# Moving the key sums, the PE transposes and the last batch's transposes of an attention + gated convolution kernel

## The chip, the cores and the metric

One core of a Trainium2 chip runs the whole program. The metric is device time in microseconds (us) for one execution, lower is better. The engines are TensorE (PE, with its weight loads shown apart as PEld), VectorE (DVE), ScalarE (ACT), GpSimd (POOL) and SyncE (SP, which here issues every DMA). Each engine works through its own queue in order.

## The reference

Attention of 12288 queries on 768 pooled keys per batch (4 batches, 128 channels), and behind it a causal 5-tap convolution that gates a projection.

```
kv_flat = mean of kv over 4 x 4 blocks, @ w_sr      # (B, 768, 128); k = v = kv_flat
s = (q @ k^T) / sqrt(128);  a = softmax(s);  x = a @ v            # (B, 12288, 128)
gate = sigmoid(sum_k conv_w[k] * x shifted by 4 - k rows)
out = (gate * (x @ w_val)) @ w_out
```

The inputs are float32 except the last weights, which can come as float64 and are then converted on DVE in 14 short steps.

## The kernel before, in words

The queries are cut into 96 groups of 512 (24 per batch), each group into four tiles j = 0 to 3 of 128 queries. The main loop runs over t = 4 * group + j and writes every engine's instructions out in that order (the order is by hand; nothing is rescheduled). At step t the current group `cur` has its softmax, while earlier groups are further on: `last` (one back) gets its normalisation row, `avg` (two back) is multiplied with the values, `xg` (three back) is convolved, `mg` (four back) is gated and projected, `og` (five back) is stored.

Per group, with the short names that the prediction uses:

- S, `score`: six matmuls that make the scores of the next tile in PSUM (three buffers, tile `s`). q and the keys are split in two parts (qh, ql and kh, kl), hence three products on two halves.
- nm, `row_max` (DVE): the negated maximum of a tile. Then `expo` (ACT), the exponential, with the row sums in z.
- `p_hi` (ACT) and `p_lo` (DVE): the exponentials as two float16 parts. For tiles 0 to 2 they go to `hl`, and DMA transposes turn them into `pt` (tiles 0 and 1 together, tile 2 alone). Tile 3 goes another way: `expo` writes it to `pf`, six PE transposes ("turns", T; T1 is the first) put it back in PSUM turned round, and `p_hi`, `p_lo` write `pt` directly.
- AV, `av_part`: 18 matmuls of `pt` with the values into one PSUM bank `av`, cut over the four steps by AV_CUTS. Then `g_x` (DVE) makes x from it, with the row `rb` of reciprocals that went by way of DRAM (`norm_turn` on PE into the bank `m`, `norm_store` copies it to r and stores rd, `norm_rows` loads rb). POOL copies the four halo columns of x first, behind `g_ql`.
- `g_qh` (ACT) and `g_ql` (POOL), at j = 2: the two parts of q for the group after the next.
- V, `g_val`: x times w_val, at j = 1, into the same single bank `m` that r was read from. h, `g_h` (DVE): (tanh + 1) times V. O, `g_out`: h times w_out, at j = 2. The convolution, `g_conv`, is on POOL but for one tap on ACT; `g_evac` on ACT writes the output tile.

The keys of the next batch are made beside the groups of the current one by `setup_steps`: one step a group, at j = 3. A step is a function that may return two more, `high` and `low`, which the loop calls at j = 0 of the next group. For 16 groups a step loads a piece of kv (the first step loads three) and its `low` is `pool_kv`, a DVE sum over the 16 pixels of a block; then come two steps of `project` (with the copies kh and vt as `high`, kl as `low`), and five of `value_steps` (the column scale, dripped over several steps by `trickle`, and the values vh and vl).

Behind the loop the last five groups n5 to n1 are finished in an order of their own, the last two with the convolution on DVE (`conv_dve`), the very last in two halves.

Of the kernel before, what the change touches and what calls it, by code (L numbers as in the profile page):

```python
# [6 lines left out]
F32 = mybir.dt.float32  # L7
# [20 lines left out]
def attn_moe_kernel(ctx, tc, qT, kvT, w_sr, w_moe, outT):  # L28
# [10 lines left out]
    TAPS = NW - 2 * C  # L39
    HALO = TAPS - 1  # L40
    PIECES = 16
    AV_CUTS = (0, 7, 9, 12, 18)
    assert 3 * NCH == AV_CUTS[-1]
    PC = NK // PIECES
    AHEAD = 5
# [17 lines left out]
    def misc():  # L63
        return ps_m.tile([P, GQ], F32, name="m")
# [55 lines left out]
    def pool_kv(st, i):  # L120
        nc.vector.tensor_reduce(out=st["pool"][:, i * PC:(i + 1) * PC],  # L121
                                in_=st.pop(("kv", i)).rearrange("c (k s) -> c k s", s=RR),
                                axis=AX.X, op=ALU.add)
# [77 lines left out]
    def setup_steps(b, st):  # L201
        def piece(i):
            if i == 0:
                key_tiles(st)
            for k in range(3) if i == 0 else (i + 2,):
                if k < PIECES:
                    load_kv(b, st, k)
            return None, lambda: pool_kv(st, i)

        steps = [lambda i=i: piece(i) for i in range(PIECES)]  # L210
        steps += [lambda h=h: project(st, h, misc()) or split_keys(st, h) for h in range(2)]
        return steps + value_steps(st)

# [27 lines left out]
    def halves(a):  # L241
        return a.rearrange("p (h k) -> p h k", h=2)
# [13 lines left out]
        nc.vector.tensor_reduce(out=nm, in_=g.s[j], axis=AX.XY, op=ALU.max, negate=True)  # L256
        g.nm[j] = nm

    def on_pe(j):

        return j >= NX

    def expo(g, j):
        if j == 0:
            g.z = zs[g.i % len(zs)]
        if on_pe(j):
            g.pf[j] = pfp.tile([P, NK], F32, name="pf")
        nc.scalar.activation(out=halves(g.pf[j]) if on_pe(j) else g.s[j], in_=g.s[j],  # L268
                             func=AF.Exp, bias=g.nm.pop(j), accum_out=g.z[:, j:j + 1])

    def norm_eps(g):
# [21 lines left out]
    def turn(g, j):  # L293

        pf = g.pf.pop(j)
        for k in range(NCH):
            c = k % (NCH // 2) * P
            nc.tensor.transpose(g.s[j][:, k // (NCH // 2), c:c + P], pf[:, k * P:(k + 1) * P],  # L298
                                ident)
# [5 lines left out]

    def part(g, j, a):

        if on_pe(j):
            return pt_tile(g)[:, j, a * NCH:(a + 1) * NCH].rearrange("p (h k) q -> p h (k q)", h=2)
        if g.hl is None:  # L310
            g.hl = hlp.tile([P, NX, 2, NK], F16, name="hl")
        return halves(g.hl[:, j, a])

    def p_hi(g, j):
# [2 lines left out]
    def p_lo(g, j):  # L317

        nc.vector.scalar_tensor_tensor(out=part(g, j, 1), in0=g.s.pop(j), scalar=2.0 ** 15,  # L319
                                       in1=part(g, j, 0), op0=ALU.mult, op1=ALU.subtract)  # L320
        if j in (1, 2):
            j0 = 0 if j == 1 else j
            nc.sync.dma_start_transpose(
                out=pt_tile(g)[:, j0:j + 1].rearrange("p j k q -> p (j k) q"),
                in_=g.hl[:, j0:j + 1].rearrange("p j a k -> p (j a k)"))
# [6 lines left out]
            nc.tensor.matmul(out, g.st[v][:, k * P:(k + 1) * P], g.pt[:, j0:j1, a * NCH + k],  # L332
                             start=(i == 0), stop=(i == len(AV_ORDER) - 1))

    def av_part(g, part):
        if part == 0:
            g.av = ps_av.tile([C, GQ], F32, name="av")
        av_range(g, g.av, AV_CUTS[part], AV_CUTS[part + 1])

    def new_x(g, prev, copy):  # L340
        g.x = xp.tile([C, HALO + GQ], F32, name="x")
# [99 lines left out]
    for i in range(PIECES):  # L441
        if i + AHEAD < PIECES:
            load_kv(0, st, i + AHEAD)
        if i == 3:
            convert = load_moe()
        pool_kv(st, i)
        if i >= 8 and convert:
            convert.pop(0)()
        if i == 3 * PIECES // 4:
            low()  # L450
        if i % (PIECES // 2) == PIECES // 2 - 1:
            h = 2 * i // PIECES
# [17 lines left out]
    for t in range(NT * G):  # L470
        gi, j = divmod(t, NT)
        cur, prev, nxt = (at(u // NT) for u in (t, t - 1, t + 1))
        last, avg, xg, mg, og = (at(gi - d) for d in (1, 2, 3, 4, 5))
        if j == 2 and gi % 2 == 0 and at(gi + 4):
            load_pair(at(gi + 4), at(gi + 5))
        if gi % NG == 1 and j == 0 and at(gi + NG - 1):
            steps += setup_steps(cur.b + 1, states[cur.b + 1])
        if t == NT + 2:
            trickle += convert

        if nxt:
            score(nxt, (j + 1) % NT)
        if mg and j == 1:
            mg.m = g_val(mg, misc())
        if mg and j == 2:
            mg.m = g_out(mg.h, misc())
        if avg:
            av_part(avg, j)

        if high and (j == 0 or t < NT):  # L490
            high()
            high = None
        row_max(cur, j)
# [24 lines left out]
        drip()
        if mg and j == 1:
# [45 lines left out]
    new_x(n1, n2, nc.scalar.copy)
    avs = [bank()[:, :half] for _ in cuts]
# [5 lines left out]
    ths = []  # L572
    n1.th = work.tile([C, GQ], F32, name="th")
    for av, c in zip(avs, cuts):
        g_x(n1, av, *c)
        ths.append(g_tanh(conv_dve(n1, *c), n1.th[:, c[0]:c[1]]))
# [3 lines left out]
    n3.th = g_tanh(n3.gate)  # L580
    h = g_h(n3.th, n3.m)
    ms = [g_val(n1, bank()[:, :half], *c) for c in cuts]
    hs = [g_h(th, m) for th, m in zip(ths, ms)]
    n3.m = g_out(h, misc())
# [33 lines left out]
```

## Time and profile before

| | us |
|---|---|
| median of 3 runs | 1132.18 (1131.02 to 1132.25) |
| the profiled execution | 1133.22, its span 1131.4 |
| busy: PE, DVE, ACT, POOL | 1063.6, 919.0, 910.4, 864.4 |
| granted PE clock, mean | 0.983 |
| bytes moved by DMA | 215.53 MB, queue share 85.4% of 16 engines |

The span runs from the first instruction to the last; the profiled execution's time is 1.8 us longer than it. In rows of the timeline the columns are the start, the length, the engine, the line, the operation, output and input, the shape, and in brackets the idle time of the engine before it and what ended that idle time. In rows of the waits: who waited for whom, the total, the number of times and the longest. In rows of the chain of waits: start, length, engine, what is written, the line and the number of instructions. Matmuls are pipelined, so the lengths in the timeline overlap; the distance between starts is what PE spends.

### The profile page before, as it was taken

The numbers are of one execution on the slowest core, as the hardware profiler recorded it, in microseconds if no ns is written. First come the engines' busy times: TensorE is split into PE (matmuls) and PEld (weight loads), VectorE is DVE, ScalarE is ACT, GpSimd is POOL, SyncE is SP. The second block draws the span as 40 slices with busy tenths as digits, with TensorE's granted clock in tenths as the row PEclk, the third lists the DMA queues.
The fourth block names the chain that finished last, engine by engine and source line by source line (L and its number), as shares of the span: only waits on it lengthen the run. The fifth ranks groups of instructions, "written<-read, shape, count | busy, mean of one in ns | idle before, by whom it ended". The sixth has DMA issues, their size and how long they took to land.

```text
span 1131.4 us, 16595 instructions
## 1 busy us (share of the span) xinstructions
PE 1063.6 (94%) x5174; PEld 715.6 (63%) x5174; DVE 919.0 (81%) x1290; ACT 910.4 (80%) x1659; POOL 864.4 (76%) x948
## 2 busy tenths in 40 slices
PE   2879999999979999999997999999999999999996
PEld 1656666666756666666764666666666666666663
DVE  6868888888858888888885888888888888888884
ACT  1868888888858888888885888888888888888881
POOL 1168788878858888888885888887888888888872
PEclk9989999999989999999998999999999999999998
DMA  7779999887879999888876999898788888888872
GB/s 271 145 178 200 211 210 232 192 178 191 187 169 198 202 224 214 206 177 191 187 165 170 209 217 226 200 221 183 171 171 197 187 170 202 186 170 199 175 148 93
DMA packets 487095, 215.53 MB, mean 190 GB/s; under 512 B 453088, under 2 KB 453856, under 8 KB 487008
## 3 DMA queue, kind: packets, MB, share of 16 engines
q1 hardware_dynamic: 487008, 214.48, 85.4%
q8 instruction: 41, 0.67, 0.2%
q14 instruction: 46, 0.38, 0.1%
HBM read 75.83 MB, written 25.36 MB: 89 GB/s over the span
## 4 chain that ended last, share of the span: by engine, by line
PE 49%; DVE 25%; ACT 11%; issue 6%; POOL 5%; DMA 3%; SPq 1%; DVEq 0%; ACTq 0%
PE s L250 17%; PE av L332 16%; PE m L388 8%; DVE nm L256 8%; POOL ql L236 5%; ACT s L268 5%; DVE pool L121 4%; DVE pt L319 4%; ACT hl L315 4%; DVE x L349 4%; PE m L398 3%; PE s L298 3%; DMA kvt<-in_kv 3%; ACT qh L232 2%; DVE h L393 2%
## 5 line engine op out<-in xcount | busy, mean ns | idle before, releaser
L368 POOL TENSOR_TENSOR sum<-sum,tap 128x512 f32<-128x512 f32 x282 | 359.6, 1275 | 39.7 <-ACT tap L357 17.8
L332 PE MATMUL av<-pt,vh 128*128 128x512 f16 x1140 | 389.1, 383 | 0.0
L256 DVE TENSOR_REDUCE nm<-s 128x1 f32<-128x768 f32 x384 | 364.4, 949 | 3.7 <-PE s L250 3.7
L268 ACT ACTIVATE s<-s,nm 128x768 f32<-128x768 f32 x288 | 251.9, 875 | 125.5 <-DVE nm L256 124.3
L359 POOL TENSOR_SCALAR tap<-x,wm 128x512 f32<-128x512 f32 x376 | 253.4, 693 | 82.4 <-DVE x L349 80.9
L319 DVE SCALAR_TENSOR_TENSOR hl<-s,hl 128x768 f16<-128x768 f32 x288 | 273.1, 948 | 21.0 <-ACT hl L315 20.3
L250 PE MATMUL s<-kh,qh 128*128 128x384 f32 x768 | 253.3, 411 | 10.8 <-DVE hl L319 8.1
L315 ACT ACTIVATE hl<-s 128x768 f16<-128x768 f32 x288 | 233.3, 810 | 9.1
L332 PEld LDWEIGHTS <-vh 128*128 128x128 f16 x1164 | 114.0, 98 | 175.5 <-issue 85.8
L332 PE MATMUL av<-pt,vl 128*128 128x512 f16 x570 | 217.5, 382 | 0.0
L236 POOL TENSOR_TENSOR ql<-q,qh 128x512 fp32r<-128x512 f32 x96 | 121.8, 1269 | 122.6 <-ACT qh L232 122.6
L250 PE MATMUL s<-kh,ql 128*128 128x384 f32 x768 | 199.1, 341 | 0.0
L250 PE MATMUL s<-kl,qh 128*128 128x384 f32 x768 | 198.9, 340 | 0.0
L250 PEld LDWEIGHTS s<-kh,qh 128*128 128x128 f32 x768 | 132.4, 193 | 51.8 <-DVE hl L319 8.4
L349 DVE SCALAR_TENSOR_TENSOR x<-av,down,rb 128x512 f32<-128x512 f32 x95 | 71.4, 751 | 89.6 <-POOL ql L236 71.5
L250 PEld LDWEIGHTS s<-kl,qh 128*128 128x128 f32 x768 | 141.3, 190 | 0.5 <-DVE kl L147 0.5
L250 PEld LDWEIGHTS s<-kh,ql 128*128 128x128 f32 x768 | 140.9, 190 | 0.0
L388 PE MATMUL m<-x,wm 128*128 128x512 f32 x188 | 103.0, 630 | 25.0 <-DVE r L285 24.9
L368 POOL TENSOR_TENSOR sum<-tap,tap 128x512 f32<-128x512 f32 x94 | 120.4, 1281 | 0.0
L393 DVE SCALAR_TENSOR_TENSOR h<-th,m 128x512 f32<-128x512 f32 x94 | 64.7, 689 | 59.2 <-PE m L388 57.7
L315 ACT ACTIVATE pt<-s 128x768 f16<-128x768 f32 x96 | 77.8, 810 | 37.8 <-PE s L298 37.8
L332 PEld LDWEIGHTS <-vl 128*128 128x128 f16 x582 | 57.6, 99 | 77.9 <-issue 55.2
(68 smaller groups left out, 1068.9 us busy)
## 6 DMA issues: line engine op xcount, KB each, us to landing
kvt<-in_kv SPq DMA_DIRECT2D x64, 384.0 KB
rb<-rd SPq DMA_DIRECT2D x96, 256.0 KB
q<-in_q SPq DMA_DIRECT2D x47, 512.0 KB
out<-o SPq DMA_DIRECT2D x46, 512.0 KB
pt<-hl SPq DMA_TRANSPOSE x192
rd<-r SPq DMA_DIRECT2D x96, 2.0 KB
out<-o SPq DMA_DIRECT2D x3, 256.0 KB
q<-in_q SPq DMA_DIRECT2D x2, 256.0 KB
```

The lines of the kernel that those rows point to most:

```text
L236: nc.gpsimd.tensor_tensor(out=g.ql, in0=g.q, in1=g.qh.bitcast(F32), op=ALU.subtract)
L250: nc.tensor.matmul(s[:, h, :HALF], a[:, sl], k[:, h * HALF:(h + 1) * HALF], start=(i == 0), stop=(i == 2))
L256: nc.vector.tensor_reduce(out=nm, in_=g.s[j], axis=AX.XY, op=ALU.max, negate=True)
L268: nc.scalar.activation(out=halves(g.pf[j]) if on_pe(j) else g.s[j], in_=g.s[j], func=AF.Exp, bias=g.nm.pop(j), accum_out=g.z[:, j:j + 1])
L315: nc.scalar.activation(out=part(g, j, 0), in_=g.s[j], func=AF.Copy, scale=2.0 ** 15)
L319: nc.vector.scalar_tensor_tensor(out=part(g, j, 1), in0=g.s.pop(j), scalar=2.0 ** 15, in1=part(g, j, 0), op0=ALU.mult, op1=ALU.subtract)
L332: nc.tensor.matmul(out, g.st[v][:, k * P:(k + 1) * P], g.pt[:, j0:j1, a * NCH + k], start=(i == 0), stop=(i == len(AV_ORDER) - 1))
L349: nc.vector.scalar_tensor_tensor(out=g.x[:, HALO + c0:HALO + c1], in0=av, scalar=g.st["down"], in1=g.rb[:, c0:c1], op0=ALU.mult, op1=ALU.mult)
L359: eng.tensor_scalar(out=g.tap[k], in0=src, scalar1=w, scalar2=1.0, op0=ALU.mult, op1=ALU.mult)
L368: nc.gpsimd.tensor_tensor(out=s, in0=acc, in1=g.tap[k], op=ALU.add)
L388: nc.tensor.matmul(m, wval, g.x[:, HALO + c0:HALO + c1], start=True, stop=True)
L393: nc.vector.scalar_tensor_tensor(out=h, in0=th, scalar=1.0, in1=m, op0=ALU.add, op1=ALU.mult)
```

## The change

Six things are done at once.

1. `pool_kv` is no longer the `low` of its step. The next step puts it on a list, and the loop takes one from the list at j = 2, behind `p_lo`. There is one step more in a setup, 24 instead of 23.
2. `row_max` and `expo` are written ahead of AV, and the six turns of tile 3 are no longer issued in one run behind AV: `av_part` puts one behind each of its last six matmuls. AV_CUTS become (0, 6, 8, 10, 18): six, two, two and eight matmuls at j = 0 to 3 instead of seven, two, three and six.
3. As a consequence `high` (kh and vt, or vh) stands behind the exponential of tile 0 on ACT, not ahead of it.
4. In the last batch, groups with an even number have all four tiles turned by DMA, 0 with 1 and 2 with 3. They have no turns on PE; tile 3's `p_hi` and `p_lo` write to `hl`.
5. The 14 steps of the weight conversion all drip from step t = 3 on; before, eight stood between the key sums of the startup and six from t = 6 on.
6. Behind the loop, AV of the last but one group comes first, and tanh, h and output of the third last group stand between the two halves of the last one.

```
-    AV_CUTS = (0, 7, 9, 12, 18)
+    AV_CUTS = (0, 6, 8, 10, 18)
...
             if i == 0:
                 key_tiles(st)
+            else:
+                pooling.append(lambda: pool_kv(st, i - 1))
             for k in range(3) if i == 0 else (i + 2,):
                 if k < PIECES:
                     load_kv(b, st, k)
-            return None, lambda: pool_kv(st, i)
-        steps = [lambda i=i: piece(i) for i in range(PIECES)]
+        steps = [lambda i=i: piece(i) for i in range(PIECES + 1)]
...
-        if j in (1, 2):
-            j0 = 0 if j == 1 else j
+        if (j % 2 or j == g.by_dma - 1) and not on_pe(g, j):
+            j0 = j // 2 * 2
             nc.sync.dma_start_transpose(
...
-    def av_part(g, part):
+    def av_part(g, part, between=()):
         if part == 0:
             g.av = ps_av.tile([C, GQ], F32, name="av")
-        av_range(g, g.av, AV_CUTS[part], AV_CUTS[part + 1])
+        lo, hi = AV_CUTS[part], AV_CUTS[part + 1]
+        for i in range(lo, hi):
+            av_range(g, g.av, i, i + 1)
+            if hi - i <= len(between):
+                between.pop(0)()
+        for matmul in between:
+            matmul()
...
+            g.by_dma = 4 if b == B - 1 and i % 2 == 0 else 3
...
-        if i >= 8 and convert:
-            convert.pop(0)()
...
-        if t == NT + 2:
+        if t == 3:
             trickle += convert
...
+        row_max(cur, j)
+        expo(cur, j)
+        turns = turn_steps(cur, j) if on_pe(cur, j) else []
         if avg:
-            av_part(avg, j)
+            av_part(avg, j, turns)
+        else:
+            for matmul in turns:
+                matmul()
         if high and (j == 0 or t < NT):
             high()
             high = None
-        row_max(cur, j)
-        expo(cur, j)
-        if on_pe(j):
-            turn(cur, j)
+        if j == NT - 1:
             norm_eps(cur)
...
+        if pooling and j == 2:
+            pooling.pop(0)()
...
     norm_reciprocal(n1)
-    p_lo(n1, NT - 1)
-    store_pair(n5)
+    av_part(n2, 0)
     norm_turn(n1, misc())
     n4.th = g_tanh(n4.gate)
-    norm_store(n1)
-    n4.m = g_val(n4, misc())
-    av_part(n2, 0)
-    norm_rows(n1)
     tap(n3, TAPS - 1, nc.scalar)
     g_conv(n3)
-    h = g_h(n4.th, n4.m)
+    p_lo(n1, NT - 1)
+    norm_store(n1)
+    store_pair(n5)
     for i in (1, 2, 3):
         av_part(n2, i)
+    norm_rows(n1)
+    n4.m = g_val(n4, misc())
...
-    av_range(n1, avs[0], 0, len(AV_ORDER), 0, NT // 2)
-    h = g_h(n2.th, n2.m)
-    av_range(n1, avs[1], 0, len(AV_ORDER), NT // 2, NT)
-    n3.m = g_val(n3, misc())
-    n2.m = g_out(h, bank())
...
+    g_x(n1, avs[0], *cuts[0])
+    h2 = g_h(n2.th, n2.m)
+    n2.m = g_out(h2, bank())
+    ths = [g_tanh(conv_dve(n1, *cuts[0]), n1.th[:, :half])]
+    n3.m = g_val(n3, misc())
+    n3.th = g_tanh(n3.gate)
...
+    g_x(n1, avs[1], *cuts[1])
+    h3 = g_h(n3.th, n3.m)
...
+    ths.append(g_tanh(conv_dve(n1, *cuts[1]), n1.th[:, half:]))
```

On PE, at j = 3 of a group in the middle, before: the end of the last three of the six AV matmuls, the turns in one run, and the score of tile 1 of the next group (LDWEIGHTS loads the weights of the row behind it).

```order
L332 LDWEIGHTS vl
L332 MATMUL av<-pt,vl 128x512
L332 LDWEIGHTS vh
L332 MATMUL av<-pt,vh 128x512
L298 MATMUL s<-ident,pf 128x128 x6
L250 MATMUL s<-kh,qh 128x384 x2
L250 MATMUL s<-kl,qh 128x384 x2
L250 MATMUL s<-kh,ql 128x384 x2
```

And in the change, from the score of tile 0 on:

```order
L251 MATMUL s<-kh,ql 128x384 x2
L336 LDWEIGHTS vl
L336 MATMUL av<-pt,vl 128x512
L336 LDWEIGHTS vh
L336 MATMUL av<-pt,vh 128x512
L336 LDWEIGHTS vh
L336 MATMUL av<-pt,vh 128x512
L300 MATMUL s<-ident,pf 128x128
L336 LDWEIGHTS vl
L336 MATMUL av<-pt,vl 128x512
L300 MATMUL s<-ident,pf 128x128
```

The first turn stands behind three AV matmuls instead of six, and the last behind the last AV, with five AVs between first and last.

On DVE, one group of a batch in which the next batch's keys are summed, before: from the reciprocal at j = 0 to x at j = 3.

```order
L275 RECIPROCAL z_103<-z_103 128x4
L319 SCALAR_TENSOR_TENSOR pt<-s,pt 128x768
L121 TENSOR_REDUCE pool<-kvt 128x48
L256 TENSOR_REDUCE nm<-s 128x1
L285 COPY r<-m 4x128
L319 SCALAR_TENSOR_TENSOR hl<-s,hl 128x768
L393 SCALAR_TENSOR_TENSOR h<-th,m 128x512
L256 TENSOR_REDUCE nm<-s 128x1
L319 SCALAR_TENSOR_TENSOR hl<-s,hl 128x768
L256 TENSOR_REDUCE nm<-s 128x1
L319 SCALAR_TENSOR_TENSOR hl<-s,hl 128x768
L349 SCALAR_TENSOR_TENSOR x<-av,down,rb 128x512
```

And in the change:

```order
L276 RECIPROCAL z_103<-z_103 128x4
L323 SCALAR_TENSOR_TENSOR pt<-s,pt 128x768
L257 TENSOR_REDUCE nm<-s 128x1
L286 COPY r<-m 4x128
L323 SCALAR_TENSOR_TENSOR hl<-s,hl 128x768
L404 SCALAR_TENSOR_TENSOR h<-th,m 128x512
L257 TENSOR_REDUCE nm<-s 128x1
L323 SCALAR_TENSOR_TENSOR hl<-s,hl 128x768
L120 TENSOR_REDUCE pool<-kvt 128x48
L257 TENSOR_REDUCE nm<-s 128x1
L323 SCALAR_TENSOR_TENSOR hl<-s,hl 128x768
L360 SCALAR_TENSOR_TENSOR x<-av,down,rb 128x512
```

The sum moved from ahead of nm of tile 1 and r to ahead of nm of tile 3; h stays ahead of nm of tile 2 in both.

On PE behind the loop, before: the last turns, the transpose of z, V of n4, and then AV of n2 (the last but one group).

```order
L298 MATMUL s<-ident,pf 128x128 x6
L278 MATMUL m<-ident,z_103 128x128
L388 MATMUL m<-x,wm 128x512
L332 LDWEIGHTS vh
L332 MATMUL av<-pt,vh 128x512
```

And in the change, from the last turn on:

```order
L300 MATMUL s<-ident,pf 128x128
L336 LDWEIGHTS vh
L336 MATMUL av<-pt,vh 128x512
L336 LDWEIGHTS vl
L336 MATMUL av<-pt,vl 128x512
L336 LDWEIGHTS vh
L336 MATMUL av<-pt,vh 128x512
```

AV of n2 no longer stands behind the transpose of z and V; these follow behind six and behind all 18 of its matmuls.

More of the change, by code (lines that the diff above doesn't have):

```diff
@@ L19 @@
 NT = GQ // P
-NX = 3
 class Group:
@@ L194, in attn_moe_kernel @@
     trickle = []
+    pooling = []
     def value_steps(st):
@@ L257, in row_max, with on_pe @@
         g.nm[j] = nm
-    def on_pe(j):
-        return j >= NX
+    def on_pe(g, j):
+        return j >= g.by_dma
     def expo(g, j):
@@ L265, in expo @@
             g.z = zs[g.i % len(zs)]
-        if on_pe(j):
+        if on_pe(g, j):
             g.pf[j] = pfp.tile([P, NK], F32, name="pf")
-        nc.scalar.activation(out=halves(g.pf[j]) if on_pe(j) else g.s[j], in_=g.s[j],
+        nc.scalar.activation(out=halves(g.pf[j]) if on_pe(g, j) else g.s[j], in_=g.s[j],
                              func=AF.Exp, bias=g.nm.pop(j), accum_out=g.z[:, j:j + 1])
@@ L291, in norm_rows, with turn_steps, block @@
         nc.sync.dma_start(out=g.rb, in_=row.broadcast_to([C, GQ]))
-    def turn(g, j):
+    def turn_steps(g, j):
         pf = g.pf.pop(j)
-        for k in range(NCH):
+        def block(k):
             c = k % (NCH // 2) * P
@@ L299, in turn @@
                                 ident)
+        return [lambda k=k: block(k) for k in range(NCH)]
     def pt_tile(g):
@@ L306, in part @@
     def part(g, j, a):
-        if on_pe(j):
+        if on_pe(g, j):
             return pt_tile(g)[:, j, a * NCH:(a + 1) * NCH].rearrange("p (h k) q -> p h (k q)", h=2)
         if g.hl is None:
-            g.hl = hlp.tile([P, NX, 2, NK], F16, name="hl")
+            g.hl = hlp.tile([P, NT, 2, NK], F16, name="hl")
         return halves(g.hl[:, j, a])
@@ L492, in attn_moe_kernel @@
             high = None
-        row_max(cur, j)
-        expo(cur, j)
-        if on_pe(j):
-            turn(cur, j)
+        if j == NT - 1:
             norm_eps(cur)
@@ L543, in attn_moe_kernel @@
     norm_reciprocal(n1)
-    p_lo(n1, NT - 1)
-    store_pair(n5)
+    av_part(n2, 0)
     norm_turn(n1, misc())
     n4.th = g_tanh(n4.gate)
-    norm_store(n1)
-    n4.m = g_val(n4, misc())
-    av_part(n2, 0)
-    norm_rows(n1)
     tap(n3, TAPS - 1, nc.scalar)
     g_conv(n3)
-    h = g_h(n4.th, n4.m)
+    p_lo(n1, NT - 1)
+    norm_store(n1)
+    store_pair(n5)
     for i in (1, 2, 3):
         av_part(n2, i)
+    norm_rows(n1)
+    n4.m = g_val(n4, misc())
     new_x(n2, n3, nc.scalar.copy)
     g_x(n2, n2.av)
-    n4.m = g_out(h, misc())
+    h4 = g_h(n4.th, n4.m)
     n2.m = g_val(n2, bank())
+    n4.m = g_out(h4, misc())
     out_tile(n4)
@@ L563, in attn_moe_kernel @@
     store(n4)
+    avs = [bank()[:, :half] for _ in cuts]
+    for i, av in enumerate(avs):
+        av_range(n1, av, 0, len(AV_ORDER), i * NT // 2, (i + 1) * NT // 2)
     n2.th = g_tanh(conv_dve(n2))
     new_x(n1, n2, nc.scalar.copy)
-    avs = [bank()[:, :half] for _ in cuts]
-    av_range(n1, avs[0], 0, len(AV_ORDER), 0, NT // 2)
-    h = g_h(n2.th, n2.m)
-    av_range(n1, avs[1], 0, len(AV_ORDER), NT // 2, NT)
-    n3.m = g_val(n3, misc())
-    n2.m = g_out(h, bank())
[L572 to L576, printed above, removed]
+    g_x(n1, avs[0], *cuts[0])
+    h2 = g_h(n2.th, n2.m)
+    n2.m = g_out(h2, bank())
+    n1.th = work.tile([C, GQ], F32, name="th")
+    ths = [g_tanh(conv_dve(n1, *cuts[0]), n1.th[:, :half])]
+    n3.m = g_val(n3, misc())
+    n3.th = g_tanh(n3.gate)
     out_tile(n2)
@@ L579, in attn_moe_kernel @@
     store(n2)
[L580 to L584, printed above, removed]
+    g_x(n1, avs[1], *cuts[1])
+    h3 = g_h(n3.th, n3.m)
+    ms = [g_val(n1, bank()[:, :half], *cuts[0])]
+    n3.m = g_out(h3, misc())
+    ths.append(g_tanh(conv_dve(n1, *cuts[1]), n1.th[:, half:]))
     g_evac(n3, n3.m)
     store(n3)
-    for h, c in zip(hs, cuts):
-        g_evac(n1, g_out(h, bank()[:, :half]), *c)
+    ms.append(g_val(n1, bank()[:, :half], *cuts[1]))
+    for th, m, c in zip(ths, ms, cuts):
+        g_evac(n1, g_out(g_h(th, m), bank()[:, :half]), *c)
         store(n1, *c)
```

## The prediction

> **What bounds the kernel now.** I read the stage windows first, then the group times, then the chain of waits inside one group, and last the timeline of the engines beside it. In the windows the columns are the stretch, its length, the busy time of PE, PEld, DVE, ACT and POOL, the granted clock, the DMA share and GB/s.
>
> ```profile
> 42.00:44.00 2.00, 1.30 (x6) 0.99 (x6) 2.00 (x4) 1.89 (x4) 0.00 (x0) 1.00 0.00 0
> 66.00:68.00 2.00, 0.16 (x1) 0.16 (x1) 2.00 (x4) 1.20 (x3) 0.00 (x0) 0.50 0.04 16
> 860.00:1100.00 240.00, 240.00 (x1196) 164.48 (x1195) 197.23 (x272) 210.32 (x384) 206.54 (x225) 1.00 0.83 179
> ```
>
> In the last batch PE is busy in all of 240 us, at full clock, with the DMA engines at 0.83. So this stage has nothing but PE's work in it. Other stages are read by the group: `norm_eps` writes z once a group, right behind the fourth exponential. These rows are those of groups 2, 25, 28, 41, 49, 73 and 95.
>
> ```profile
> 55.88 0.21 ACT L272 ACTIVATE z<-z 128x4 f32<-128x4 f32 x1
> 317.14 0.20 ACT L272 ACTIVATE z<-z 128x4 f32<-128x4 f32 x1
> 348.31 0.21 ACT L272 ACTIVATE z<-z 128x4 f32<-128x4 f32 x1
> 492.44 0.21 ACT L272 ACTIVATE z<-z 128x4 f32<-128x4 f32 x1
> 591.87 0.20 ACT L272 ACTIVATE z<-z 128x4 f32<-128x4 f32 x1
> 867.63 0.20 ACT L272 ACTIVATE z<-z 128x4 f32<-128x4 f32 x1
> 1100.81 0.21 ACT L272 ACTIVATE z<-z 128x4 f32<-128x4 f32 x1
> ```
>
> Groups 29 to 41 (13 of them, each with one key sum of the next batch) took 144.13 us, 11.09 each. Groups 74 to 95 (22, without key sums) took 233.18 us, 10.60 each. The three segments between them are 3 to 25 (261.26 us), 26 to 49 (274.73) and 50 to 73 (275.76). The chain of waits in the last batch names only PE lines:
>
> ```profile
> 984.90 0.66 PE s L298 x6
> 985.55 1.05 PE s L250 x6
> 986.60 1.53 PE av L332 x7
> ...
> 989.31 0.86 PE m L388 x2
> ...
> 994.20 1.31 PE av L332 x6
> 995.51 0.66 PE s L298 x6
> ```
>
> From turns to turns it is 10.61 us. The unit prices follow: six score matmuls (S) 1.05, one AV matmul 1.31/6 = 0.218, six turns 0.66, so 0.11 each, the value matmul (V) 0.86. But PE being full does not say how much slack the other engines have. The timeline of the same group tells that:
>
> ```profile
> 985.00 0.75 DVE L349 SCALAR_TENSOR_TENSOR x<-av,down,rb 128x512 f32<-128x512 f32 x1 [0.87 <-POOL ql L236]
> 985.67 0.95 DVE L256 TENSOR_REDUCE nm<-s 128x1 f32<-128x768 f32 x1
> 987.46 0.95 DVE L256 TENSOR_REDUCE nm<-s 128x1 f32<-128x768 f32 x1
> 988.33 0.27 DVE L285 COPY r<-m 4x128 f32<-4x128 f32 x1
> 989.15 1.02 PE L388 MATMUL m<-x,wm 128*128 128x512 f32 x2
> 990.27 0.69 DVE L393 SCALAR_TENSOR_TENSOR h<-th,m 128x512 f32<-128x512 f32 x1 [0.80 <-PE m L388]
> 990.88 0.95 DVE L256 TENSOR_REDUCE nm<-s 128x1 f32<-128x768 f32 x1
> 991.92 0.88 ACT L268 ACTIVATE s<-s,nm 128x768 f32<-128x768 f32 x1 [0.58 <-DVE nm L256]
> 992.95 0.81 ACT L315 ACTIVATE hl<-s 128x768 f16<-128x768 f32 x1
> 993.65 0.61 ACT L232 CAST qh<-q 128x512 fp32r<-128x512 f32 x1
> 994.16 0.90 ACT L268 ACTIVATE pf<-s,nm 128x768 f32<-128x768 f32 x1
> 995.21 0.72 PEld L298 LDWEIGHTS s<-ident,pf 128*128 128x128 f32 x6 [0.19 <-ACT pf L268]
> 995.35 0.82 PE L298 MATMUL s<-ident,pf 128*128 128x128 f32 x6
> ```
>
> Read it downwards. h waited for V (0.80 idle), the row maximum nm of tile 2 stands behind h on DVE, ACT waited for that nm (0.58 idle), and its next three instructions run without a gap up to pf, which the turns transpose. The turns' weight load waited 0.19 for pf. From the start of V to the first turn (T1) these steps are 1.12 + 0.61 + 1.04 + 1.03 + 0.70 + 0.51 + 1.05 + 0.14 = 6.20 us, all latency. PE's own work between the two is V 0.86, two AVs, S, the out matmul (O, 0.86 as V), three AVs, S, six AVs: 6.21 us. The slack is nil: PE reaches the turns just when pf is there.
>
> Groups with a key sum close the same loop at another place:
>
> ```profile
> 450.97 0.94 DVE L121 TENSOR_REDUCE pool<-kvt 128x48 f32<-128x768 f32 x1
> 452.69 0.27 DVE L285 COPY r<-m 4x128 f32<-4x128 f32 x1
> 453.02 1.12 PE L388 MATMUL m<-x,wm 128*128 128x512 f32 x2 [0.20 <-DVE r L285]
> 454.25 0.69 DVE L393 SCALAR_TENSOR_TENSOR h<-th,m 128x512 f32<-128x512 f32 x1 [0.42 <-PE m L388]
> ```
>
> The sum stands ahead of nm of tile 1 and r there; V waits for r (they share one PSUM bank) and h comes 1.23 us behind a V that waited, not 1.12. That is why these groups take 11.09.
>
> **The change, part by part.** *Turns between the AV matmuls.* AV_CUTS move two AVs of a group from before the last score to behind it, and of the eight now there only three stand ahead of T1. PE's work from V to T1 falls to 0.86 + 2 AV + 1.05 + 0.86 + 2 AV + 1.05 + 3 AV = 5.35 us (7 AV are 1.53). pf is not earlier: no instruction of the chain h, nm, exponential, hl, qh, pf is moved. So PE waits about 0.87 us at T1 in every group with turns. Queued behind T1 on PE are five AVs and five turns, and for the last AV waits x on DVE, for the last turn p_hi of tile 3 on ACT. The wait is not given back, since the loop closes through V. In the new order it is, from T1: five turns and four AVs to the last AV 0.55 + 0.87 = 1.42; last AV to x 0.48, by these rows of the tail, where x waits for an AV:
>
> ```profile
> 1100.83 0.87 PE L298 MATMUL s<-ident,pf 128*128 128x128 f32 x6 [0.25 <-ACT pf L268]
> 1110.10 0.38 PE L332 MATMUL av<-pt,vh 128*128 128x512 f16 x1
> 1110.58 0.75 DVE L349 SCALAR_TENSOR_TENSOR x<-av,down,rb 128x512 f32<-128x512 f32 x1 [4.88 <-PE av L332]
> ```
>
> Then x to nm of tile 0 0.67, to nm of tile 1 1.79 (reciprocal and p_lo of tile 3 lie between), to r 0.87, to V 0.33 by the rows of 452.69 and 453.02. That is 5.56 us to V, which has waited for r, and 6.20 + 0.11 = 6.31 on to the next T1. **Loop: 11.87 us a group**, against 10.61. Before, x came 0.26 behind T1 (985.00 against 984.74, T1 less one period) and had to wait for POOL only; now it comes 1.90 behind. If V finds r ready the loop is 0.11 shorter; if x costs nothing it is 6.20 plus PE's own 5.27 from T1 to V (1.42 + the last AV and turn 0.33 + S + 6 AV + S + the small z transpose), 11.47. These are the lower ends; I take 11.87, as the rows of a V behind r are those of 45 groups.
>
> A rule of the Trainium skill speaks for the interleaving: the page "TensorE: Matmul & The Clock Gate", section "Wait — 56ns, not 53.3ns?", gives 55.6 ns for 128 warm columns, and its section "Step-by-step: what each phase is for" says that weight loads are pulled ahead of running matmuls, which stay in program order. By it a turn hidden between AVs would cost half of the 0.11 of the row, the loop would be 0.27 shorter, and the whole sum some 22 us less. The trace cannot separate the two, since in the run of six the loads take 0.72/6 = 0.12 each, as long as the turns; in the new order a turn has to hide the next AV's load, so I keep 0.11.
>
> *Key sums.* They leave the place ahead of r and come one group later, at j = 2, between p_lo of tile 1 and nm of tile 3. The stall on kv goes:
>
> ```profile
> DVE pool L121 <- DMA kvt<-in_kv: 25.2, 8, 7.0
> DVE kl L147 <- ACT vt L144: 2.4, 1, 2.4
> ```
>
> Five of the eight waits are short and lie in the startup; three of 6 to 7 us (the longest is in the row) fall in the second group of a setup; the sum now stands more than a period behind its load. What is late next is nm of tile 3: three DVE steps of 0.87 (nm to r, 987.46 to 988.33) and 0.98 on to ACT are 3.59 us from nm of tile 2 to pf, where ACT's own steps are 3.28: 0.31 us later, and with rounding 0.30. **Groups with a sum: 12.17 us**, 16 per batch.
>
> *kh, vt, vh behind the exponential.* kl waits for vt in the startup (second row above), and its place on DVE is ahead of nm of tile 1. From nm of tile 0: 1.04 to the exponential, 1.03 for it, some 0.9 for kh and vt and 0.5 for kl (estimates from half a nm each, on half as many columns) make 3.4 where 1.79 stood: two groups per batch at about 13.5. vh and vl likewise, 13.05 twice. The group with the column scale gets about 12.9 (one 0.86 maximum ahead of p_lo), the three plain ones 11.87. A batch is 16 x 12.17 + 2 x 13.5 + 2 x 13.05 + 12.9 + 3 x 11.87 = 296 us.
>
> *Segments.* Groups 3 to 25: 284 (one plain group fewer, no V in group 3) against 261.3, +22.4. Groups 26 to 49: +21.5. Groups 50 to 73: +19.0 (group 72 gains 1.4, next part). These already contain the stalls that go.
>
> *All four tiles by DMA in twelve even groups.* No turns, so no wait for pf. x follows V by way of PE: V 0.86, 2 AV, S, O, 2 AV, S, 7 AV, x 0.48, in all 6.70; then 0.67 + 1.79 + 0.87 + 0.33 to V: 10.4. A pair of groups is 10.4 + 11.87 = 22.27 against 21.2: eleven pairs, +11.8. The transposes of tiles 2 and 3 come four steps later than that of tile 2 did and are read a period later still; the DMA share would go from 0.83 to about 0.9. rd of the next group is queued behind them on SP, but x needs rb only a period later. Cost nothing; if it did not hold, one late transpose a pair would be added to the wait at AV, 0 to 2 us a pair.
>
> *Conversion of the weights.* Fourteen short DVE steps leave the key sums of the startup and go into the first groups:
>
> ```profile
> 16.37 0.29 DVE L90 TENSOR_SCALAR rest<-rest 128x261 int32<-128x261 int32 x1
> ```
>
> Each takes 0.2 us before the next starts (16.57). Six stand between sums that end the startup, -1.2 at most if the loads keep up; eight more now stand in groups whose DVE is full, +1.6 at most. I take 0.
>
> *Tail.* AV of the group before the last started behind p_lo, r and a V; x came 9.75 us behind T1 (1100.83 to 1110.58). Now: 1.42 + 0.48 + x itself 0.75 to free the bank + 18 AV 3.9 + 0.5 = 7.1, so -2.6. The last two DVE chains and the tanh of the third last group go between each other; of the 20.8 us behind that x I give 2 more. -4.6, between 0 and -8.
>
> **Sum**: 1133.2 (the profiled execution: the span below and 1.8 around it; 1.0 above the median of the runs) + 22.4 + 21.5 + 19.0 + 11.8 - 4.6 = 1203.3; against the median 1202.
>
> ```profile
> span 1131.4 us, 16595 instructions
> ```
>
> **Rivals.** (1) *PE never waits at T1* (the other side). If pf came within 5.35 us of V, the groups would stay on PE's work: sum groups 10.62 instead of 11.09, stalls gone (segments -14, -16, -17), even groups 10.2 (-4), tail -4.6: 1076. For it speaks only that PE is the one engine without idle; against it stand the 0.80, 0.58 and 0.19 us that h, nm and the weight load waited. It decides at V to T1 = 5.35. (2) *Turns cost half and x nothing*: 0.055 for a turn, the middle between nothing and the row, takes 0.27 off 11.47; loop 11.2, sum groups 11.5, about 55 us less than my sum, 1148. Against it: the tail's x, which did wait for an AV. (3) *The clock falls.* The rows of 42 and 66 show the granted clock at 1.00 with 0.70 us of idle in 2 us, and at 0.50 behind the 6 us stall. If 1.3 us of idle a group brought it down in part, PE's work would grow: V takes twice as long then, and groups of 13 us would give some 1290. The page "TensorE: Matmul & The Clock Gate" of the Trainium skill has a section on it, "A second HAM failure mode: psum-queue depth-cycling": short idles between bursts can make the clock swing; its ordinary rule asks for 3.4 us of idle, which agrees with the row at 42. (4) *No change*: gains and waits would have to cancel, a wait of 0.2 a group instead of 1.2.
>
> **How the numbers follow.** Forecast 0.82, and its own range 1175 to 1222: 11.6 to 12.1 a group over some 80 groups is -22 to +18. Rival 1 0.08, rival 2 0.05, rival 3 0.04, rival 4 0.01. The range 1160 to 1224 leaves out rivals 1 and 3, most of rival 2 and the ends of the forecast. What can be told from no change is 0.2%, 2.3 us: faster 0.08 (rival 1), same 0.01 (rival 4), slower 0.91.
>
> **What would show it.** Right: turns' weight load idle on pf at 0.8 us a group (0.2 now); r to V still a wait in most groups; z to z near 11.9 in groups without a sum and 12.2 with one, alternating 11.9 and 10.4 at the end; no wait of DVE on kv behind the startup; x waiting for AV, not for POOL. Wrong: z to z at 10.6, a PE without idle, or a granted clock below 0.95 in the middle.

## The result, and the profile after

The changed kernel took 1197.68 us (median of 4 runs, 1196.84 to 1197.89), the kernel before 1132.22 on the same chip. The ratio is 1.058 (95%: 1.056 to 1.060): slower by 65 us. The profiled execution took 1196.84.

From the page of the changed kernel, its span, its busy times and the chain of waits by engine:

```profile
span 1195.1 us, 16476 instructions
...
PE 1080.4 (90%) x5102; PEld 698.7 (58%) x5102; DVE 916.5 (77%) x1290; ACT 909.6 (76%) x1659; POOL 864.8 (72%) x948
...
POOL 31%; issue 17%; DVE 17%; PE 17%; ACT 15%; DMA 2%; POOLq 0%; SPq 0%; DVEq 0%; ACTq 0%
```

No engine is full and no engine owns the chain: POOL has 31% of it, and DVE, PE and ACT 15% to 17% each. That is how a loop over several engines looks (that POOL's share is named too high is shown further down). (PE's busy time is 17 us longer although it has 72 turns fewer; matmuls are pipelined and their ends modelled, so it is no measure of work.)

The z rows of the same groups as in the prediction, 2, 25, 28, 41, 49, 73 and 95:

```profile
56.51 0.20 ACT L273 ACTIVATE z<-z 128x4 f32<-128x4 f32 x1
335.89 0.20 ACT L273 ACTIVATE z<-z 128x4 f32<-128x4 f32 x1
372.60 0.21 ACT L273 ACTIVATE z<-z 128x4 f32<-128x4 f32 x1
529.64 0.21 ACT L273 ACTIVATE z<-z 128x4 f32<-128x4 f32 x1
629.44 0.21 ACT L273 ACTIVATE z<-z 128x4 f32<-128x4 f32 x1
921.84 0.21 ACT L273 ACTIVATE z<-z 128x4 f32<-128x4 f32 x1
1168.57 0.20 ACT L273 ACTIVATE z<-z 128x4 f32<-128x4 f32 x1
```

| stretch | before | after | difference | predicted |
|---|---|---|---|---|
| start to z of group 2 | 55.88 | 56.51 | +0.63 | 0 |
| groups 3 to 25 | 261.26 | 279.38 | +18.12 | +22.4 |
| groups 26 to 49 | 274.73 | 293.55 | +18.82 | +21.5 |
| groups 50 to 73 | 275.76 | 292.40 | +16.64 | +19.0 |
| groups 74 to 95 | 233.18 | 246.73 | +13.55 | +11.8 |
| behind z of group 95 | 30.59 | 26.53 | -4.06 | -4.6 |

The sum is 63.70, the whole difference of the spans. The loss lies in every group, also in those of the last batch that have no key sum. A plain group takes 11.77 us from z to z (10.61 before). Groups 29 to 41, each with a key sum, take 157.04/13 = 12.08, one of them 12.41 and the others 12.05 (11.09 before).

The waits of the changed kernel (who waits for whom: total, times, longest):

```profile
PEld s L300 <- ACT pf L269: 95.8, 84, 1.6
DVE x L360 <- PE s L300: 69.5, 29, 2.4
...
PE s L300 <- ACT pf L269: 54.8, 84, 1.1
...
DVE pool L120 <- DMA kvt<-in_kv: 5.3, 6, 2.6
```

The stall on kv is gone, 25.2 to 5.3. In its place the weight load of the first turn waits for pf in all 84 groups with turns, 95.8 us in all, 1.14 each (PE itself stood idle for 0.65 of it, 54.8 in all). The timeline of group 48, cut to the loop, shows how that wait comes back on itself:

```profile
604.80 0.33 PE L300 MATMUL s<-ident,pf 128*128 128x128 f32 x1 [0.49 <-ACT pf L269]
605.18 0.27 PE L300 MATMUL s<-ident,pf 128*128 128x128 f32 x1
...
606.27 0.38 PE L336 MATMUL av<-pt,vh 128*128 128x512 f16 x1
...
606.75 0.75 DVE L360 SCALAR_TENSOR_TENSOR x<-av,down,rb 128x512 f32<-128x512 f32 x1 [2.42 <-PE s L300]
...
608.37 0.93 DVE L323 SCALAR_TENSOR_TENSOR pt<-s,pt 128x768 f16<-128x768 f32 x1
...
609.35 0.30 PEld L251 LDWEIGHTS s<-kh,qh 128*128 128x128 f32 x2 [0.46 <-DVE pt L323]
...
610.08 0.27 DVE L286 COPY r<-m 4x128 f32<-4x128 f32 x1
...
610.50 1.02 PE L399 MATMUL m<-x,wm 128*128 128x512 f32 x2
...
611.63 0.69 DVE L404 SCALAR_TENSOR_TENSOR h<-th,m 128x512 f32<-128x512 f32 x1 [0.41 <-ACT s L269]
...
612.24 0.95 DVE L257 TENSOR_REDUCE nm<-s 128x1 f32<-128x768 f32 x1
613.28 0.88 ACT L269 ACTIVATE s<-s,nm 128x768 f32<-128x768 f32 x1 [0.20 <-DVE nm L257]
614.30 0.81 ACT L319 ACTIVATE hl<-s 128x768 f16<-128x768 f32 x1
615.01 0.61 ACT L233 CAST qh<-q 128x512 fp32r<-128x512 f32 x1
615.52 0.90 ACT L269 ACTIVATE pf<-s,nm 128x768 f32<-128x768 f32 x1
616.57 0.33 PE L300 MATMUL s<-ident,pf 128*128 128x128 f32 x1 [0.48 <-ACT pf L269]
```

From T1 (604.80) the last AV comes 1.47 later, x 0.48 behind it. x, 0.67 long on DVE's queue, pushes back nm of tile 0, p_lo of tile 3 (608.37) and r. The score at 609.35 waits for that p_lo (0.46), since it writes over the bank that p_lo reads; V follows at 610.50. Then h, nm, exponential, hl, qh and pf run without a gap to the next T1 at 616.57, 11.77 behind the first. Ahead of it PE stood idle for 0.48. The row of h names ACT's exponential as what ended its wait, but h starts 1.12 to 1.14 behind V in 87 of its 97 rows, whether ACT or V is named, and 1.12 behind it in the group of the kernel before that the prediction shows; by these distances it is V that h waits for.

In the last batch the groups alternate, 10.56 and 11.77 here, which is the DMA variant beside the one with turns:

```profile
1001.76 0.20 ACT L273 ACTIVATE z<-z 128x4 f32<-128x4 f32 x1
1012.32 0.20 ACT L273 ACTIVATE z<-z 128x4 f32<-128x4 f32 x1
1024.09 0.21 ACT L273 ACTIVATE z<-z 128x4 f32<-128x4 f32 x1
```

### The profile page after: what moved, and what is told of

Same layout as the page of the kernel before. It is cut to its first block, busy times and chain, and to the rows that moved or that the text cites. A ratio compares the mean times of both kernels' runs of the same rounds, so it can differ in the third digit from the quotient of the medians.

```text
span 1195.1 us, 16476 instructions
## 1 busy us (share of the span) xinstructions
PE 1080.4 (90%) x5102; PEld 698.7 (58%) x5102; DVE 916.5 (77%) x1290; ACT 909.6 (76%) x1659; POOL 864.8 (72%) x948
## 4 chain that ended last, share of the span: by engine, by line
POOL 31%; issue 17%; DVE 17%; PE 17%; ACT 15%; DMA 2%; POOLq 0%; SPq 0%; DVEq 0%; ACTq 0%
POOL sum L379 15%; POOL tap L370 10%; DVE x L360 6%; PE av L336 5%; PE s L251 5%; POOL ql L237 5%; DVE nm L257 5%; ACT s L269 5%; ACT hl L319 4%; ACT pf L269 3%; PE s L300 3%; PE m L399 2%; DVE h L404 2%; ACT qh L233 1%; DMA kvt<-in_kv 1%
## 5 line engine op out<-in xcount | busy, mean ns | idle before, releaser
L336 PE MATMUL av<-pt,vh 128*128 128x512 f16 x1140 | 380.0, 380 | 0.9 <-DVE x L360 0.8
L269 ACT ACTIVATE s<-s,nm 128x768 f32<-128x768 f32 x300 | 261.8, 873 | 114.4 <-DVE nm L257 101.6
L323 DVE SCALAR_TENSOR_TENSOR hl<-s,hl 128x768 f16<-128x768 f32 x300 | 284.3, 948 | 10.0 <-ACT hl L319 10.0
L251 PE MATMUL s<-kh,qh 128*128 128x384 f32 x768 | 245.9, 401 | 20.0 <-DVE hl L323 6.8
L319 ACT ACTIVATE hl<-s 128x768 f16<-128x768 f32 x300 | 243.2, 811 | 8.7
L300 PE MATMUL s<-ident,pf 128*128 128x128 f32 x504 | 140.5, 282 | 54.8 <-ACT pf L269 54.8
L251 PEld LDWEIGHTS s<-kh,qh 128*128 128x128 f32 x768 | 125.4, 191 | 102.2 <-DVE pt L323 30.9
L319 ACT ACTIVATE pt<-s 128x768 f16<-128x768 f32 x84 | 68.0, 810 | 111.0 <-PE s L300 111.0
L300 PEld LDWEIGHTS s<-ident,pf 128*128 128x128 f32 x504 | 70.5, 141 | 100.5 <-ACT pf L269 95.8
L336 PEld LDWEIGHTS <-vl 128*128 128x128 f16 x582 | 61.6, 106 | 67.4 <-issue 46.8
```

Of the source, the lines that this page charges most:

```text
L251: nc.tensor.matmul(s[:, h, :HALF], a[:, sl], k[:, h * HALF:(h + 1) * HALF], start=(i == 0), stop=(i == 2))
L269: nc.scalar.activation(out=halves(g.pf[j]) if on_pe(g, j) else g.s[j], in_=g.s[j], func=AF.Exp, bias=g.nm.pop(j), accum_out=g.z[:, j:j + 1])
L319: nc.scalar.activation(out=part(g, j, 0), in_=g.s[j], func=AF.Copy, scale=2.0 ** 15)
```

## The experiments

The kernel before took 1133.05 us beside the runs of the first four, 1133.63 beside the next four and 1133.19 beside the last. "Groups" are distances from z to z.

**1. The turns in one run again.** The changed kernel with all else kept, AV_CUTS too:

```
-            av_part(avg, j, turns)
-        else:
-            for matmul in turns:
-                matmul()
+            av_part(avg, j)
+        for matmul in turns:
+            matmul()
```

> The changed kernel, but with the six turns in one run behind all eight AV matmuls of j = 3 (cuts, key sums, DMA tiles and tail as changed). Theory (T1 waits for pf, and x behind the last AV closes the loop): PE then reaches T1 6.4 us behind V, later than pf is there (6.2), so the wait goes and groups run at PE's 10.6; 107 us less than the changed kernel, 1090 us (1078 to 1102). Rival (the wait is not due to the interleaving, but to the new place of the key sums or the new cuts): still near 1198, at least above before.

Measured 1093.67, ratio to before 0.965 (0.964 to 0.966). Sum groups and plain groups both take 10.68. Its waits:

```profile
DVE x L360 <- PE av L336: 49.0, 43, 1.2
...
PEld s L300 <- ACT pf L269: 11.2, 51, 1.2
```

The wait for pf falls from 95.8 to 11.2. So the place of six matmuls, with nothing added or taken away, is worth 104 us and decides the sign of the whole change.

**2. The new order of the turns alone.** The kernel before, with the new AV_CUTS and the turns between the AVs; key sums, conversion, DMA tiles and tail stay. The core of the edit:

```
-    AV_CUTS = (0, 7, 9, 12, 18)
+    AV_CUTS = (0, 6, 8, 10, 18)
...
-        if avg:
-            av_part(avg, j)
...
+        turns = turn_steps(cur, j) if on_pe(j) else []
+        if avg:
+            av_part(avg, j, turns)
+        else:
+            for matmul in turns:
+                matmul()
         if on_pe(j):
-            turn(cur, j)
```

> The kernel before with the new cuts and the turns between the last AV matmuls, nothing else. Theory: plain groups at the 11.77 us of the changed kernel, groups with a sum 0.87 more (the sum still stands ahead of r, inside the loop), 12.64; stalls on kv stay; in all some 121 us more than before, 1253 us (1235 to 1265). Rival (the sum of several mishaps, the turns only part of it): between 1140 and 1200.

Measured 1251.47, ratio 1.104 (1.103 to 1.106). Plain groups take 11.77, the same as in the full change: the loop does not depend on the key sums. Groups with a sum at its old place take 12.63 (12.64 expected), and the stalls on kv stay (18.6 and 19.0 in groups 26 and 50).

**3. The key sums alone.** The kernel before, with the sums on the list and at j = 2 behind p_lo:

```
+            else:
+                pooling.append(lambda: pool_kv(st, i - 1))
...
-            return None, lambda: pool_kv(st, i)
+        steps = [lambda i=i: piece(i) for i in range(PIECES + 1)]
...
+        if pooling and j == 2:
+            pooling.pop(0)()
```

> The kernel before with the key sums moved to j = 2 one group later, nothing else. Theory: the three stalls on kv go, groups with a sum at 10.9 (pf 0.3 us late, no slack at T1) instead of 11.09; 1099 us (1088 to 1110). Rival (the loads are late anyway, or the delayed pf takes back what the stall gives): 1125 to 1135.

Measured 1093.25, ratio 0.965 (0.964 to 0.966), 6 us under what was expected. The z rows of groups 28 and 41:

```profile
338.26 0.20 ACT L274 ACTIVATE z<-z 128x4 f32<-128x4 f32 x1
...
478.99 0.21 ACT L274 ACTIVATE z<-z 128x4 f32<-128x4 f32 x1
```

140.73/13 = 10.83 for a sum group, against 11.09 before and 10.9 expected. Groups 26 and 50 take 11.32 instead of 18.80 and 19.15, and the ones behind them 10.61 instead of 12.37 and 13.06. This part is a clear gain of 40 us; in the full change the loop covers it.

**4. The loop, made shorter at another place.** The changed kernel with `g_qh` and `g_ql` moved from j = 2 to behind the exponential that writes pf, in groups with turns:

```
+            if at(gi + 2) and cur.by_dma < NT:
+                g_qh(at(gi + 2))
+                g_ql(at(gi + 2))
...
-        if at(gi + 2) and j == 2:
+        if at(gi + 2) and j == 2 and cur.by_dma == NT:
```

> The changed kernel, with qh and ql behind pf instead of ahead of it in the groups that have turns. Theory (the loop through pf on ACT): 0.51 us less in each group with turns and without a key sum (11.77 to 11.26), nothing in groups with a sum, whose pf waits for nm of tile 3 on DVE (12.05 stays): some 17 us less, 1180 us (1174 to 1186). Rival (the interleaving itself costs PE time, or only x behind the last AV sets the pace): no change, 1197.

Measured 1181.75, ratio 1.043 (1.041 to 1.045). The end of a plain group, from its timeline:

```profile
318.72 0.81 ACT L319 ACTIVATE hl<-s 128x768 f16<-128x768 f32 x1
319.42 0.90 ACT L269 ACTIVATE pf<-s,nm 128x768 f32<-128x768 f32 x1
...
320.30 0.62 ACT L233 CAST qh<-q 128x512 fp32r<-128x512 f32 x1
```

pf follows hl at once, 0.70 behind its start instead of 1.22. Plain groups take 11.25, down by 0.52, which is qh's slot and nothing else. Sum groups stay at 12.05: there pf waits for DVE, not for ACT, as this row of the changed kernel shows:

```profile
552.73 0.90 ACT L269 ACTIVATE pf<-s,nm 128x768 f32<-128x768 f32 x1 [0.19 <-DVE nm L257]
```

In the last batch, too, a pair of groups takes 21.84 instead of 22.34. So what a group lasts is the length of the loop. PE's work is the same in this run and in the full change.

**5. The tail alone.** The kernel before, with AV of n2 first and n3's tanh, h and output between the last halves (point 6 of the change, its lines as in the diff there):

> The kernel before with the new order behind the loop, nothing else. Theory: what the changed kernel's tail is shorter by (26.5 us behind the last z against 30.6), 4 us: 1129 us (1127 to 1131). Rival (part of that was the DMA turns of the last but one group): 1131 to 1133.

Measured 1129.15, ratio 0.9962 (0.9949 to 0.9974): by this ratio 4.3 us less. In its profiled execution the stretch behind the last z (1100.48, of a span of 1125.5) is 25.02 us, against 30.59 before and 26.53 in the full change.

**6. The DMA tiles alone.** The kernel before with four tiles by DMA in the even groups of the last batch:

```
+            g.by_dma = 4 if b == B - 1 and i % 2 == 0 else 3
...
-        if j in (1, 2):
-            j0 = 0 if j == 1 else j
+        if (j % 2 or j == g.by_dma - 1) and not on_pe(g, j):
+            j0 = j // 2 * 2
```

> The kernel before with all four tiles of the even groups of the last batch turned by DMA, nothing else. Theory: an even group saves six turns (0.66) of PE but then waits for the loop x, nm, r, V, h, qh, ql, x, some 10.2 us; a pair 20.8 instead of 21.2, 5 us in all: 1128 us (1125 to 1131). Rival (V behind x behind the last AV, as in the changed kernel): nothing, 1133.

Measured 1128.53, ratio 0.9959 (0.9945 to 0.9973), by this ratio 4.6 us less. Groups alternate between 10.28 and 10.61, so only half of the six turns' 0.66 is saved. In an even group x is now late:

```profile
961.13 1.26 POOL L235 TENSOR_TENSOR ql<-q,qh 128x512 fp32r<-128x512 f32 x1 [0.40 <-ACT qh L231]
...
962.40 0.75 DVE L348 SCALAR_TENSOR_TENSOR x<-av,down,rb 128x512 f32<-128x512 f32 x1 [0.87 <-POOL ql L235]
...
964.01 0.93 DVE L318 SCALAR_TENSOR_TENSOR hl<-s,hl 128x768 f16<-128x768 f32 x1
...
965.06 0.30 PEld L249 LDWEIGHTS s<-kh,qh 128*128 128x128 f32 x2 [0.40 <-PE m L277]
```

What x holds up is again the score, by way of p_lo. PE, with six matmuls fewer, comes to the score of tile 2 before p_lo of tile 3 (964.01), which stands behind x on DVE, has read the bank that this score writes. The last row names PE's transpose of z, but in all twelve even groups the score's weight load starts 0.11 or 0.12 behind the end of p_lo, and so it does in the even groups of the full change, where the transpose of z starts 0.54 ahead of it instead of 0.33 and the score's first matmul names p_lo (at 1005.17, 0.30). V starts 1.49 behind the transpose of z here (964.73 to 966.22) and 1.16 in the odd group ahead of it (954.77 to 955.93); this 0.33 is the half that is lost. x itself waits for POOL, which waits for qh on ACT. That x waited 0.87 for ql before too (row 985.00 of the prediction), but PE had no idle time behind it then. Behind the last z the profiled execution takes 28.71 us instead of 30.59, so part of the gain lies there.

**7. All but the new order of turns and `high`.** The changed kernel with AV_CUTS, the run of turns and the place of `high` as before:

```
-    AV_CUTS = (0, 6, 8, 10, 18)
+    AV_CUTS = (0, 7, 9, 12, 18)
...
+        if high and (j == 0 or t < NT):
+            high()
+            high = None
...
-            av_part(avg, j, turns)
+            av_part(avg, j)
+        for matmul in turns:
+            matmul()
...
-        if high and (j == 0 or t < NT):
-            high()
-            high = None
```

> The changed kernel with the turns and the cuts of before and with kh, vt and vh ahead of the exponential again; key sums, DMA tiles and tail stay. Theory: the parts add: 1093 (sums alone) less 4 for the tail and 5 for the DMA tiles, 1084 us (1080 to 1090). Rival: the DMA tiles give nothing, 1089.

Measured 1087.28, ratio 0.960 (0.958 to 0.961), under the 1089 of the rival by which the DMA tiles would give nothing. The DMA tiles do give something: groups 74 to 95 take 230.24 instead of the 233.90 of experiment 3. The parts nearly add: 1093.25 with the sums, less 4.3 and 4.6, is 1084.3, 3 us under what was measured. These 3 us do not lie in the conversion at t = 3: groups 1 and 2 take 9.93 and 10.31 instead of 9.31 and 9.70, but group 0 ends earlier by as much, and the z of group 2 comes at 56.32, in experiment 3 at 56.31. They lie behind the last z, where the new order alone saves 5.57 (5), the DMA tiles alone 1.88 (6), and both together 4.47 (26.12 instead of 30.59).

**8. The sum one step later.** As 7, with the sum taken from the list at j = 3:

```
-        if pooling and j == 2:
+        if pooling and j == 3:
```

> As the kernel with the turns of before, and with the key sum at j = 3 ahead of x, where DVE sat idle 0.87 us for POOL, instead of j = 2. Theory: nm of tile 3 is early again, groups with a sum at PE's 10.62 instead of 10.83, 45 of them: 9 us less than it, 1075 us (1071 to 1081). Rival (the sum delays x and with it r and V): no gain or a loss of up to 10 us.

Measured 1078.28, ratio to before 0.951 (0.950 to 0.953). From its page:

```profile
PE 1039.8 (97%) x5102; PEld 707.8 (66%) x5102; DVE 919.6 (85%) x1290; ACT 903.7 (84%) x1659; POOL 865.1 (80%) x948
...
PE 90%; DVE 4%; ACT 3%; DMA 2%; issue 1%; POOL 0%; SPq 0%; DVEq 0%; ACTq 0%
```

From z to z a sum group now takes 10.61, as long as a plain one. PE owns 90% of the chain. This version beats both kernels.

**9. The turns two AVs earlier.** The changed kernel with the turns behind the first six of the eight AVs at j = 3, not the last six:

```
-            if hi - i <= len(between):
+            if between:
```

> The changed kernel with the six turns behind the first six of the eight AV matmuls of j = 3 instead of the last six. Theory (PE waits at T1 until pf is there, then does what stands between T1 and the last AV, and x closes the loop): 0.55 us more stand between them (1.97 instead of 1.42), so each of 82 groups with turns takes 0.55 more, 12.32 and 12.60: 1243 us (1235 to 1250). Rival (only the number of interleaved turns matters, not where they stand): 1197.

Measured 1245.92, ratio 1.100 (1.098 to 1.102). Plain groups take 12.36 (12.32 expected). T1 stands behind one AV only, and between T1 and the last AV are five turns and six AVs:

```profile
325.09 0.33 PE L300 MATMUL s<-ident,pf 128*128 128x128 f32 x1 [0.92 <-ACT pf L269]
...
327.10 0.38 PE L336 MATMUL av<-pt,vh 128*128 128x512 f16 x1
...
327.58 0.75 DVE L360 SCALAR_TENSOR_TENSOR x<-av,down,rb 128x512 f32<-128x512 f32 x1 [2.95 <-PE av L336]
...
337.45 0.33 PE L300 MATMUL s<-ident,pf 128*128 128x128 f32 x1 [0.92 <-ACT pf L269]
```

From T1 to the last AV is 2.01 instead of 1.47, and the period grows by 0.59. x follows the last AV by 0.48 as before, although the last turn now stands ahead of two AVs: it is the last AV that x waits for. PE reaches T1 earlier and only waits longer, 0.92 instead of 0.49.

## Why the prediction was right

The forecast of 1202 stands against 1197.68. Point by point:

**The wait at T1 and the loop.** Shown. The weight load waits for pf in every group with turns, the clock stays, and the period follows the loop wherever it was cut or stretched: 0.52 out of ACT's part takes 0.52 off (4), 0.54 more on PE adds 0.59 (9), and with the turns in one run a plain group takes 10.68 and 10.61 (1, 7). The size was 11.77 instead of 11.87, nearly what the prediction named for a V that finds r ready (0.11 shorter). In the timeline above r is done at 610.35 and V starts at 610.50 behind the score's six matmuls, so it was not r that held V, but the score, which waited for p_lo of tile 3. This step the prediction does not have, and one of its signs, a wait of V for r in most groups, did not come: no V of the loop waits for r. By the 0.33 taken V would have started at 610.41, 0.09 earlier; that the way by p_lo and the score is nearly as long as the way by r is luck. It also splits PE's idle time: at T1 the turn waits 0.48 here and 0.65 in the mean, not the 0.87 reckoned, and the score's weight load waits 0.46. From V to h it is then 1.13, as behind a V that did not wait, not the 1.23 taken. The other differences are small: T1 to last AV 1.47 (1.42 taken), r to V 0.42 (0.33), pf to T1 1.05 (1.19 taken with the 0.14 of the weight load, which now starts in the same row time as T1). Together +0.05 + 0.09 - 0.10 - 0.14 = -0.10.

**The price of a turn.** Between AVs the turns come 0.325 apart (605.18 to 606.48 are four steps, 1.30). Less the 0.218 of an AV that is 0.11 each, what it cost in the run of six. The page "TensorE: Matmul & The Clock Gate" of the Trainium skill, section "Wait — 56ns, not 53.3ns?", gives 0.056 for a matmul of 128 columns, without a word on float32 transposes such as these. No run here shows a turn at that price, and the measurement decides. Rival 2, which rested on half-price turns and an x without cost, gave 1148 and is refuted by both of its halves: x waited for PE in this loop.

**Sum groups.** Predicted 12.17, measured 12.05, the same 0.1 too high. The 0.30 by which the sum makes nm of tile 3 late came out as 12.05 - 11.77 = 0.28. The chain of waits misleads here: it names POOL's copy of the halo columns and 1.70 of "issue" ahead of x. These rows are the copy, the last turn and x of one sum group:

```profile
553.83 0.19 POOL L356 COPY x<-x 128x4 f32<-128x4 f32 x1
...
555.46 0.27 PE L300 MATMUL s<-ident,pf 128*128 128x128 f32 x1
...
555.73 0.75 DVE L360 SCALAR_TENSOR_TENSOR x<-av,down,rb 128x512 f32<-128x512 f32 x1 [2.17 <-issue]
```

The copy had ended 1.71 us before x started, and x starts 0.27 behind the last turn's start, as in the plain group (606.48 and 606.75). By these distances it was PE that released x; POOL's 31% of the chain is too high by such steps.

**kh, vt, vh behind the exponential.** 13.30 (13.5 predicted) and 12.90 (13.05); the column scale 12.68 (12.9). Together with the loop's 0.1 these are why the three segments came out 2.4 to 4.3 lower each. What the order of `high` costs can be read between experiments 1 and 7, which differ in AV_CUTS as well: 11.76, 12.05, 11.65 against 11.31, 11.28, 11.32 in groups 20 and 21 (kh) and 25 (vh).

**The last batch.** A pair takes 22.34 (22.27). The DMA group was 10.57 instead of 10.4, since here too V stands behind the score that p_lo holds (0.48 behind r, 1005.80 to 1006.28, where 0.33 was taken), and the segment +13.5 instead of +11.8. That the late transposes cost nothing held: no wait of PE for a DMA is among the waits.

**The start.** +0.6, between the -1.2 and +1.6 of the bounds. Group 0 ends 1.2 earlier, groups 1 and 2 take 1.9 more. Experiment 7 beside 3 (56.32 and 56.31) shows no cost of the conversion by itself.

**The tail.** -4.1 in the full change, -4.6 predicted. The near hit hides two things. The DMA tiles, for which the prediction has nothing here, shorten this stretch too, and the two do not add (experiment 7). And the step behind the number failed in part: x of n2 does come 7.4 us behind T1, as reckoned (7.1), yet it waits for rb, not for AV. The rows of the last T1 and x:

```profile
1168.59 0.33 PE L300 MATMUL s<-ident,pf 128*128 128x128 f32 x1 [1.11 <-ACT pf L269]
...
1176.03 0.75 DVE L360 SCALAR_TENSOR_TENSOR x<-av,down,rb 128x512 f32<-128x512 f32 x1 [2.80 <-DMA rb<-rd]
```

The way of the reciprocals by DRAM is what an even earlier AV would run into.

**The other rivals.** Rival 1 (PE never waits, 1076) needed pf 5.35 us behind V; it came 6.07 behind (610.50 to 616.57). Its time is that of a kernel without the loop, and experiment 8 reaches 1078 in this way, by the old order. Rival 3 (the clock): the stretch 540 to 600 has 6.09 us of PE idle in 60, spread over five groups, at a granted clock of 1.00. Columns as in the prediction's windows:

```profile
540.00:600.00 60.00, 53.91 (x256) 34.43 (x254) 44.11 (x67) 45.32 (x85) 42.58 (x49) 1.00 0.71 156
```

So waits of about a microsecond a group left the clock alone. Rival 4 would have needed the key sums' 40 us and the loop's loss to cancel; the loss is three times the gain (118 us in experiment 2).

## What to carry to other kernels

An engine that is busy all the time tells nothing of the slack of the others: before instructions are moved on it, follow one value round the engines (here V, h, nm, exponential, pf, turns, AV, x, V), add up its latencies, and compare the sum with the period; if they are equal, putting an early consumer further ahead on PE only makes PE wait, and delaying what closes the loop lengthens every period. Take a bundle of edits apart before judging it: of this one the key sums gave 40 us, the tail and the DMA tiles 4 to 5 each by themselves, and the interleaving, which moved six matmuls, took all of it and 65 us more. A sum of inputs that stalls an engine costs less a period later and at a place where nothing of the loop stands behind it.

## What the runs showed of the hardware that was not expected

In the tail a DVE tap took twice as long beside POOL's additions. The taps on DVE and the last additions on POOL, first of the changed kernel and then of the kernel before:

```profile
1177.29 1.07 DVE L385 TENSOR_SCALAR fast<-x,wm 128x512 f32<-128x512 f32 x1
...
1175.47 4.02 POOL L379 TENSOR_TENSOR sum<-sum,tap 128x512 f32<-128x512 f32 x3
```

```profile
1111.44 0.49 DVE L374 TENSOR_SCALAR fast<-x,wm 128x512 f32<-128x512 f32 x1
...
1105.71 3.94 POOL L368 TENSOR_TENSOR sum<-sum,tap 128x512 f32<-128x512 f32 x3
```

In the changed kernel POOL's additions reach to 1179.49 and the tap lies within them: 1.07 us. In the kernel before they had ended 1.8 us before it: 0.49. In experiments 5 and 8, where the two meet for 0.05 and 0.26 us, it took 0.48 and 0.54. In experiments 2, 4 and 9, where they run on for 0.84, 2.08 and 2.39 us behind its start, it took 1.12, 0.95 and 1.26. That the one slows the other was not tried by itself; the runs show that they come together.
